# The last output tile of an attention and gMLP block in two column halves, and six earlier stores split in two

## The chip, the core and the metric

The kernel runs on one core of a Trainium2 chip. The core has five engines, each with its own queue of instructions: TensorE (PE; its weight loads are shown apart as PEld), VectorE (DVE), ScalarE (ACT), GpSimd (POOL) and SyncE (SP). Sixteen DMA engines move data between the chip's memory (HBM) and the core's (SBUF), and TensorE writes its results to a third memory, PSUM. The metric is the device time of one execution in microseconds (us), the median of several runs; less is better.

## The reference

There are two parts, one behind the other, for 4 batches of 768 positions. First attention with 8 heads of 64 columns, in which a position sees the first 4 positions and the 128 up to itself:

```python
keep = is_sink | in_window
scores = np.where(keep, scale * np.matmul(q, k.transpose(0, 1, 3, 2)), -1e9)
x = softmax(scores) @ v                        # -> [4, 768, 512]
```

Then a gated block over the attention's output `x`:

```python
h = gelu(x @ w_in)                             # [4, 768, 1024]
u, v = h[..., :512], h[..., 512:]
v_n = (v - mean(v)) / sqrt(var(v) + 1e-6) * g_ln
v_s = np.einsum('ts,bsd->btd', w_sg, v_n) + b_sg[None, :, None]
out = x + (u * v_s) @ w_out                    # float32 [4, 768, 512]
```

## The kernel before, in words

All work is written as small steps, and the string `STEPS` (lines 20 to 68) names them in the order in which they are recorded: `AV.3.1.0` is a function `AV` with the arguments 3, 1 and 0. The loop at lines 674 to 679 calls them one after the other. Nothing reorders them: each engine's queue holds its instructions in the order of the string, and the compiler's framework adds the semaphore waits that the data need. The batches overlap, so that the attention of one stands between the gated steps of the batch before it.

What the change touches is the end of a batch. A batch `b` has six output tiles `t`, of 128 positions and 512 columns each:

- `SP` (line 626, TensorE) multiplies by `w_sg`, `GT` (line 631, VectorE) scales and adds the bias, and `GM` (line 636, VectorE or GpSimd) multiplies by `u`. This gives the gated operand `wsg_gated`, one slot for three tiles.
- `OU` (line 643, TensorE) is the last product of a tile: four matmuls of 512 columns, added up in one tile `mm` of 128x512 float32 in PSUM. There are four such tiles in turn.
- `RA` (line 647, VectorE) adds `x` and writes a tile `ot` of 128x512 float32 in SBUF. There are six such tiles in turn, so an add of one batch waits until the store of the tile before in the same buffer is done.
- `ST` (line 666, SyncE) stores `ot` to the output, 256 KB in 128 rows of 2 KB.

For batch 2 the stores are recorded in the order 0, 1, 3, 2, 4, 5. For batch 3, which ends the kernel, the products are recorded in the order 3, 4, 0, 1, 2, 5, each followed by its add and its store; there is no other work left beside them.

Three functions for halves of a tile stand in the kernel already but are not called by its `STEPS`: `OH` (line 652) multiplies one half of the columns, `RH` (line 659) adds it and `SH` (line 662) stores it:

```python
    def cols(h):
        return slice(d_model // 2 * h, d_model // 2 * (h + 1))

    def OH(b, t, h):
        hf, tl = t // 3, t % 3
        ps = mm_ring["o", b, t] if h else fresh(mm_ring, ("o", b, t))
        for dc in range(KU):
            nc.tensor.matmul(ps[:, cols(h)], gated(b, hf)[:, dc, 128 * tl:128 * (tl + 1)],
                             w_out_sb[:, dc, cols(h)], start=(dc == 0), stop=(dc == KU - 1))
```

The DMAs that SyncE issues use eight completion semaphores in turn: the first DMA has number 0, the ninth has number 0 again. Each DMA instruction first waits until the DMA that had its semaphore before is done. When all steps are recorded, the framework adds closing code (shown at line 710, the launch): SyncE waits for all completion semaphores one after the other, then a barrier of all engines ends the program.

Of the kernel before, what the change touches and what calls it, by code (L numbers as in the profile page):

```python
# [58 lines left out]
MK.3.1.2.P GT.2.1.2 AV.3.1.0 NR.3.0.0 AV.3.2.0 AV.3.3.0 MK.3.0.2.P NR.3.1.0 QK.3.2.2 QK.3.3.2 EX.3.2.2 SP.2.0.2  # L59
NR.3.2.0 NR.3.3.0 EX.3.3.2 TBL.G SP.2.0.3 MK.3.2.2.P GT.2.0.2 XD.3.0 AV.3.0.1 GT.2.0.3 MK.3.3.2.P AV.3.1.1 NR.3.0.1  # L60
AV.3.2.1 GM.2.0.3.P NR.3.1.1 AV.3.3.1 SP.2.1.3 GM.2.0.2.D GM.2.1.1.P NR.3.2.1 OU.2.0 NR.3.3.1 GT.2.1.3 XD.3.1 OU.2.1
RA.2.0 GM.2.1.3.P OU.2.2 GM.2.1.2.D ST.2.0 RA.2.1 MV.3.0 RA.2.2 ST.2.1 OU.2.3 GV.3.0 OU.2.4 BN.3.0 MV.3.1 RA.2.3
RA.2.4 MV.3.2 ST.2.3 GV.3.1 ST.2.2 ST.2.4 BN.3.1 OU.2.5 GV.3.2 MU.3.2 BN.3.2 RS.3.1 MU.3.1 GU.3.2 NM.3.1 RS.3.2 NM.3.2
Z.3.0.D Z.3.1.A MU.3.0 Z.3.2.D Z.3.3.A Z.3.4.A Z.3.5.D RA.2.5 ST.2.5 SP.3.1.0 GU.3.0 SP.3.1.1 GU.3.1 GT.3.1.0 SP.3.1.2
GM.3.1.0.D GT.3.1.1 SP.3.1.3 GM.3.1.1.D GT.3.1.2 SP.3.0.0 GM.3.1.2.D SP.3.0.1 GT.3.0.0 GT.3.1.3 SP.3.0.2 GT.3.0.1
GM.3.1.3.P SP.3.0.3 GM.3.0.0.D GM.3.0.1.P GT.3.0.2 OU.3.3 GM.3.0.2.D GT.3.0.3 OU.3.4 GM.3.0.3.D RA.3.3 OU.3.0 RA.3.4
ST.3.3 OU.3.1 RA.3.0 ST.3.4 OU.3.2 ST.3.0 RA.3.1 OU.3.5 ST.3.1 RA.3.2 ST.3.2 RA.3.5 ST.3.5
"""


# [644 lines left out]
```

## Time and profile before

| what | value |
|---|---|
| three runs | 156.55, 156.59 and 156.74 us; median 156.59 |
| span of the profiled execution, first to last instruction | 154.68 us |
| SyncE's DMAs by the page: stores of the output | 24, 256 KB each, 2.3 us (median) from issue to landing |
| SyncE's DMAs: all | 49 |
| longest wait of SyncE's queue for an add (L666 for L647) | 9.8 us |
| output matmuls L643, 128x512 | 96, 379 ns recorded for one |
| adds L647, 128x512 | 24, 683 ns mean |
| granted TensorE clock, mean | 0.997 |

The profile is of one execution. Its span has its own clock, from the first instruction to the last; the runs are device times of whole executions, which is why they are longer. The three run times do not say which of them, if any, is the profiled one. A matmul's recorded time overlaps the next one's, so 379 ns is not what one costs in a row of them. "DMA to landing" is from the issue of a DMA on its queue to the last of its sixteen landings, one for each DMA engine. The view of the closing line lists event semaphores, which are waits, and drains, which wait for an engine to be empty.

### The profile page before, as it was taken

The page shows a single profiled execution, that of the slowest core. Times are in us where ns is not written, and L with a number is a line of the kernel's source. Part 1 is how long each engine was busy: PE and PEld are TensorE (multiplying, and loading weights), DVE is VectorE, ACT ScalarE, POOL GpSimd, SP SyncE. Part 2 cuts the span into 40 slices and gives each one's busy share as a digit, 9 for nine tenths or more (in the row PEclk, how much of TensorE's full clock was granted, in tenths as well). Part 3 has the DMA queues.
Part 4 walks back from the last instruction along what each step waited for, and adds up shares of the span by engine and source line. Part 5 has one row for each costly group of instructions (what it writes and reads, how often), then busy time and mean ns, then how long its engine had stood idle before and what let it go on. Part 6 is the DMA issues. An engine that isn't in the chain of part 4 may idle for free.

```text
span 154.7 us, 3863 instructions
## 1 busy us (share of the span) xinstructions
PE 147.4 (95%) x1550; PEld 94.6 (61%) x1550; DVE 123.2 (80%) x295; ACT 99.9 (65%) x117; POOL 99.3 (64%) x127
## 2 busy tenths in 40 slices
PE   6999789999999999999999999999999999999990
PEld 2455477779776776758466754585577644876530
DVE  4557789829989988897898987899799958767981
ACT  3689799699999868457987764369858022590000
POOL 4099779378999999999369769540898600400400
PEclk9999999999999999999999999999999999999998
DMA  4999999999999999999999499994610483210064
GB/s 165 295 344 157 155 195 192 169 188 190 150 144 148 186 156 173 149 154 156 157 177 252 122 277 170 192 183 58 225 72 20 86 237 112 91 72 2 0 231 177
DMA packets 86170, 24.67 MB, mean 159 GB/s; under 512 B 78660, under 2 KB 83016, under 8 KB 86152
## 3 DMA queue, kind: packets, MB, share of 16 engines
q0 software_dynamic: 64608, 11.01, 95.5%
q1 hardware_dynamic: 21544, 13.41, 32.2%
q8 instruction: 12, 0.20, 0.5%
q14 instruction: 6, 0.05, 0.1%
HBM read 24.81 MB, written 6.29 MB: 201 GB/s over the span
## 4 chain that ended last, share of the span: by engine, by line
PE 63%; POOL 18%; DMA 10%; DVE 3%; ACT 2%; issue 2%; SPq 1%; ACTq 0%
PE mm L626 17%; PE mm L643 11%; PE sc L606 10%; PE sc L565 10%; DMA v_sb<-in_v_dram 6%; POOL k L224 5%; PE sc L482 4%; DMA uT<-in_k_dram 4%; POOL q L224 4%; PE mm L523 3%; POOL wsg_gated L636 3%; PE mm L527 2%; POOL v_sb L270 2%; PE mm L381 2%; POOL P L497 2%
## 5 line engine op out<-in xcount | busy, mean ns | idle before, releaser
L487 ACT ACTIVATE P<-sc 128x1024 bf16<-128x1024 f32 (+1 forms) x48 | 43.4, 953 | 10.5 <-PE sc L482 10.4
L626 PE MATMUL mm<-wsgT,z 128*128 128x384 bf16 x192 | 34.4, 327 | 0.3 <-ACT z L596 0.3
L626 PEld LDWEIGHTS <-z 128*128 128x128 bf16 x192 | 17.6, 98 | 12.5 <-issue 0.7
L569 ACT ACTIVATE vt<-sc 128x1024 f32<-128x1024 f32 x12 | 12.3, 1026 | 18.4 <-PE sc L565 18.4
L643 PE MATMUL mm<-w_out_sb,wsg_gated 128*128 128x512 bf16 x96 | 22.7, 379 | 0.0
L631 DVE SCALAR_TENSOR_TENSOR gtmp<-mm,g_sb,b_bc 128x384 bf16<-128x384 f32 x32 | 19.0, 609 | 4.2 <-PE mm L626 4.0
L565 PE MATMUL sc<-w_in_sb,xT 128*128 128x512 bf16 x96 | 22.2, 379 | 0.0
L636 POOL TENSOR_TENSOR wsg_gated<-gtmp,uT 128x384 bf16<-128x384 bf16 x15 | 14.9, 1007 | 11.3 <-DVE gtmp L631 11.2
L606 PE MATMUL sc<-xT,w_in_sb 128*128 128x256 bf16 x192 | 22.1, 273 | 0.0
L497 POOL TENSOR_SCALAR_AFFINE_SELECT P<-P 128x512 bf16<-128x512 bf16 x21 | 13.7, 654 | 12.5 <-ACT P L487 12.5
L606 PEld LDWEIGHTS <-w_in_sb 128*128 128x128 bf16 x192 | 18.7, 98 | 3.0
L578 DVE BATCH_NORM_STATS2 st<-vt 128x6 f32<-128x512 f32 x24 | 15.4, 684 | 6.1 <-ACT vt L569 6.0
L540 DVE TENSOR_TENSOR x_sb<-mm,rcp 128x384 bf16<-128x384 f32 (+1 forms) x36 | 18.5, 513 | 1.2
L647 DVE TENSOR_TENSOR ot<-mm,x_sb 128x512 f32<-128x512 f32 x24 | 16.1, 683 | 2.0 <-PE mm L643 1.9
L587 POOL TENSOR_TENSOR rs<-rs,neg_half 128x4 f32<-128x4 f32 (+1 forms) x8 | 7.1, 883 | 15.9 <-DVE rs L582 14.5
L523 PE MATMUL mm<-v_sb,P 128*128 128x65 bf16 x192 | 15.9, 194 | 1.3 <-DMA v_sb<-in_v_dram 0.8
L224 POOL DMA_DIRECT2D k<-in_k_dram x18 | 16.4, 929 | 0.4 <-POOL wsg_gated L636 0.4
L224 POOL DMA_DIRECT2D q<-in_q_dram x18 | 16.5, 941 | 0.0
L523 PEld LDWEIGHTS <-P 128*128 128x128 bf16 x192 | 14.5, 97 | 3.2 <-issue 1.1
L611 ACT ACTIVATE uT<-sc 128x1024 bf16<-128x1024 f32 x12 | 12.2, 1022 | 5.1 <-PE sc L606 5.1
L643 PEld LDWEIGHTS <-wsg_gated 128*128 128x128 bf16 x96 | 9.2, 98 | 10.2 <-issue 0.3
L565 PEld LDWEIGHTS <-xT 128*128 128x128 bf16 x96 | 9.2, 98 | 10.1
(89 smaller groups left out, 249.4 us busy)
## 6 DMA issues: line engine op xcount, KB each, us to landing
out_dram<-ot SPq DMA_DIRECT2D x24, 256.0 KB, 2.3
v_sb<-in_v_dram POOLq DMA_DIRECT2D x8, 384.0 KB, 8.5
q<-in_q_dram POOLq DMA_DIRECT2D x18, 128.0 KB, 6.6
k<-in_k_dram POOLq DMA_DIRECT2D x18, 128.0 KB, 7.5
wsg_gated<-in_moe_w_sg_dram POOLq DMA_DIRECT2D x2, 576.0 KB, 8.4
w_in_sb<-in_moe_w_in_dram POOLq DMA_DIRECT2D x2, 512.0 KB, 10.1
uT<-in_q_dram SPq DMA_DIRECT2D x2, 384.0 KB, 3.1
uT<-in_k_dram SPq DMA_DIRECT2D x2, 384.0 KB
```

The lines of the kernel that those rows point to most:

```text
L224: return nc.gpsimd.dma_start(out=dst.rearrange("p (h d) -> p h d", h=H), in_=heads(src, b, i))
L487: nc.scalar.activation(out=P.new((b, p, g))[:, :, 0:w], in_=sc_ring[b, p, g][:, :, 0:w], func=AF.Exp, scale=scale)
L497: nc.gpsimd.affine_select(out=p4[:, :, :, 0:128], in_=p4[:, :, :, 0:128], compare_op=ALU.is_ge, fill=0.0, base=0, pattern=[[0, 2], [0, 2], ...
L523: nc.tensor.matmul(av[:, il, hl, :], pt[:, hl, c:c + 128], vb[:, h, i, :], start=first, stop=False)
L540: nc.vector.tensor_mul(x_sb.get(b)[:, i0:i0 + n, 128 * p:128 * (p + 1)].rearrange("p t (h d) -> p t h d", h=2), av[:, :, :, 0:Dh], rcp[:, ...
L565: nc.tensor.matmul(hp[:, jl, :], xT[b][:, 2 * g + jl, c, :], w_in_sb[:, c, d_half:2 * d_half], start=(c == 0), stop=(c == KD - 1))
L606: nc.tensor.matmul(hp[:, dc // 2, 256 * (dc % 2):256 * (dc % 2 + 1)], w_in_sb[:, c, 128 * dc:128 * (dc + 1)], xT[b][:, 2 * g:2 * g + 2, c, :],
L626: nc.tensor.matmul(ps[:, 0:NH], z[b][:, si, 128 * dc:128 * (dc + 1)], wsgT[:, si, NH * hf:NH * (hf + 1)], start=(si == 0), stop=(si == NT ...
L631: nc.vector.scalar_tensor_tensor(out=gtmp.new((b, hf, dc)), in0=mm_ring["g", b, hf, dc][:, 0:NH], scalar=g_sb[:, dc:dc + 1], in1=b_bc[:, N ...
L636: (nc.vector if e == "D" else nc.gpsimd).tensor_mul(gated(b, hf)[:, dc, :], gtmp[b, hf, dc], uT[b][:, dc, NH * hf:NH * (hf + 1)])
L643: nc.tensor.matmul(ps, gated(b, hf)[:, dc, 128 * tl:128 * (tl + 1)], w_out_sb[:, dc, :], start=(dc == 0), stop=(dc == KU - 1))
L647: nc.vector.tensor_add(ot.new((b, t)), mm_ring["o", b, t], x_sb[b][:, t, :])
```

## The change

Only `STEPS` changes. In batch 2 each of the six stores `ST` becomes two `SH`, one for each half of the columns, recorded one behind the other at the place of the old store. In batch 3 the last tile (tile 5) is made as two `OH`, added by two `RH` and stored by two `SH`; the two products stand one behind the other, and the first add follows the add and store of tile 2. SyncE issues 56 DMAs in place of 49. The order of all other steps stays as it is.

```diff
-RA.2.0 GM.2.1.3.P OU.2.2 GM.2.1.2.D ST.2.0 RA.2.1 MV.3.0 RA.2.2 ST.2.1 OU.2.3 GV.3.0 OU.2.4 BN.3.0 MV.3.1 RA.2.3
-RA.2.4 MV.3.2 ST.2.3 GV.3.1 ST.2.2 ST.2.4 BN.3.1 OU.2.5 GV.3.2 MU.3.2 BN.3.2 RS.3.1 MU.3.1 GU.3.2 NM.3.1 RS.3.2 NM.3.2
-Z.3.0.D Z.3.1.A MU.3.0 Z.3.2.D Z.3.3.A Z.3.4.A Z.3.5.D RA.2.5 ST.2.5 SP.3.1.0 GU.3.0 SP.3.1.1 GU.3.1 GT.3.1.0 SP.3.1.2
...
-ST.3.3 OU.3.1 RA.3.0 ST.3.4 OU.3.2 ST.3.0 RA.3.1 OU.3.5 ST.3.1 RA.3.2 ST.3.2 RA.3.5 ST.3.5
+RA.2.0 GM.2.1.3.P OU.2.2 GM.2.1.2.D SH.2.0.0 SH.2.0.1 RA.2.1 MV.3.0 RA.2.2 SH.2.1.0 SH.2.1.1 OU.2.3 GV.3.0 OU.2.4
+BN.3.0 MV.3.1 RA.2.3 RA.2.4 MV.3.2 SH.2.3.0 SH.2.3.1 GV.3.1 SH.2.2.0 SH.2.2.1 SH.2.4.0 SH.2.4.1 BN.3.1 OU.2.5 GV.3.2
+MU.3.2 BN.3.2 RS.3.1 MU.3.1 GU.3.2 NM.3.1 RS.3.2 NM.3.2 Z.3.0.D Z.3.1.A MU.3.0 Z.3.2.D Z.3.3.A Z.3.4.A Z.3.5.D RA.2.5
+SH.2.5.0 SH.2.5.1 SP.3.1.0 GU.3.0 SP.3.1.1 GU.3.1 GT.3.1.0 SP.3.1.2 GM.3.1.0.D GT.3.1.1 SP.3.1.3 GM.3.1.1.D GT.3.1.2
...
+OU.3.3 GM.3.0.2.D GT.3.0.3 OU.3.4 GM.3.0.3.D RA.3.3 OU.3.0 RA.3.4 ST.3.3 OU.3.1 RA.3.0 ST.3.4 OU.3.2 ST.3.0 RA.3.1
+OH.3.5.0 OH.3.5.1 ST.3.1 RA.3.2 ST.3.2 RH.3.5.0 SH.3.5.0 RH.3.5.1 SH.3.5.1
```

## The prediction

> **What bounds the kernel.** I read the head of the page first: which engine fills the span.
>
> ```profile
> span 154.7 us, 3863 instructions
> ...
> PE 147.4 (95%) x1550; PEld 94.6 (61%) x1550; DVE 123.2 (80%) x295; ACT 99.9 (65%) x117; POOL 99.3 (64%) x127
> ```
>
> TensorE is busy for 95% of the span, so whatever the change does beside TensorE in the middle is hidden. It must act in the tail, after the last matmul. So next I read the chain of work that ended last, for 145 to 155 us:
>
> ```profile
> 144.89 0.49 PE mm L626 x3
> 145.38 5.19 PE mm L643 x24
> 150.57 0.02 issue
> 150.59 0.69 DVE ot L647
> ```
>
> The 24 matmuls of the last six output tiles end at 150.57, and one add of 0.69 us follows. The chain stops there, at 151.28, though the span goes on to 154.68: 3.4 us come after the last computation. The view of the output tiles from 151.2 us, and the view of the closing line L710 on SyncE from 153.3 us, say what they are:
>
> ```profile
> L666 SPq DMA_DIRECT2D out_dram<-ot x1: 332/332/332, 151.3 to 151.3; - x1
> ...
> DMA to landing us min/median/max: 2.0/2.0/2.0
> ```
>
> ```profile
> L710 SPq EVENT_SEMAPHORE  x10: 17/28/28, 153.4 to 154.6; - x10
> L710 SPq DRAIN  x3: 7/7/13, 153.8 to 154.2; - x3
> ```
>
> The last store is issued at 151.313 and its sixteenth landing comes at 153.336, 2.02 us later. Then SyncE runs its closing waits: the one for the last store passes at 153.353, seven more follow 0.06 us apart, and the first drain starts at 153.847, 0.49 us after the landing was seen. From that drain to the end of the span are 0.83 us. So the tail is add 0.69, store 2.02, closing waits 0.49, final barrier 0.83.
>
> **The change part by part**, made against the span of 154.68 us. The median of the runs, 156.59 us, lies 1.91 us above it; I take this as unchanged.
>
> 1. Matmuls. Four of 512 columns become eight of 256. The new shape has a row in this trace: 48 matmuls of L606, 128x256 with a new weight load each, follow in 5.24 us, 0.109 us each. The old ones follow in 5.19 / 24 = 0.216. So 8 x 0.109 - 4 x 0.216 = +0.01 us: the last result comes at 150.60. The four extra weight loads (98 ns each on PEld) lie beside matmuls, as they do in L606; bare they would cost +0.39.
>
> 2. Adds. The order of the built program shows that the first half's add waits for TensorE and the second half's does not: TensorE counts up only once, by eight, at the eighth matmul. So the first add cannot begin while the second half is multiplied; it begins at 150.60. Its price is in the trace: L540 has 128x256 from float32 in 424 ns. So it ends at 151.02. A second add starts some 0.08 us before the first one is recorded as ended (three adds of 0.68 to 0.69 take 1.97 together), so it runs from 150.94 to 151.37, 0.09 later than the single add. On this the Trainium skill (PSUM — Partial Sum Buffer, PSUM bank collisions raise a hardware error) says to guard PSUM by bank and not by address, because TensorE writing a bank while VectorE reads it is an error. Both halves lie in one tile of 512 float32 and, by that page, in one bank; so by that rule the early start is ruled out in any build, and without it the sum would be about 0.15 us lower (third rival).
>
> 3. Issues. A store goes out 0.03 us after its add (151.28 to 151.31), so half 0 at 151.05. The next cannot follow at once: the stores at 148.29 and 148.73 stand 0.44 apart, with the second one's data ready. So half 1 goes out at 151.49, 0.18 us later than the whole tile did. No transpose stands ahead of it; the long issues of 0.83 and 0.86 us in this trace are the first stores after transposes.
>
> 4. Landing. A row becomes 1 KB in place of 2 KB. By the packet records of SyncE's queue the medians are 18 ns for 256 bytes, 27 for 512, 65 for 1536 and 85 for 2048; 1 KB is between, an estimate of 45 ns. A store is 128 rows, eight on each of 16 DMA engines, so a half saves 8 x 40 ns = 0.32 us: it lands 1.70 us after its issue, at 153.19. One DMA engine can be later: at 149.10 it takes a packet of 8192 bytes for 0.42 us (queue q14, instructions), and it ends the fifth tile's rows only at 152.35. Behind them 16 rows of 45 ns end at 153.07, and with 0.34 us from last row to landing (152.995 to 153.336 now) that is 153.41. Whether that packet comes again there is open, so I keep both ends and take the middle, 153.30: 0.04 earlier than now.
>
> 5. Closing waits. By the built program, SyncE's DMAs use eight semaphores in turn, and the closing code waits for them in the order 0 to 7. Of 49 DMAs the last is on number 0, so seven waits for long finished stores come behind it. Of 56 the last two are on 6 and 7, the last to be waited for. Behind the last landing then stands one step of 0.065 us before the drain, in place of 0.49: 0.43 us go. Nothing else is late there: VectorE's own drain ends at 151.34 and the other engines' earlier. Bounds: 0, if something unseen holds the drain, and 0.49.
>
> 6. The third batch. Six more issues of 0.39 us (the median row) and six lane waits, 2.6 us on SyncE, come between 124 and 140 us. Behind them no store is due until 147.43: SyncE's longest wait for an add is 9.8 us, and that hides them. Their data are the same bytes, while the DMA engines are at 42% (124 to 137 us) and 10% (137 to 145.2). The last batch's adds wait for these stores' buffers, which are free by about 140.1 and first wanted at 146.72. If that cover were gone it would be 0.44 us for each issue. The step is worth nothing in itself: it moves the last stores from semaphore 0 to 6 and 7.
>
> Sum: last landing 153.30, wait seen 0.02 later, one step 0.065, then 0.83: span 154.21 against 154.68, **-0.46 us, so 156.13, given as 156.1**. With the ends of step 4 it is -0.35 to -0.57, 156.0 to 156.25.
>
> **The rivals.**
>
> First, slower: an instruction block in front of the last half. The page's queue q8 carries twelve packets of 16 KB, 0.88 to 1.37 us each, on single DMA engines. The change adds 8 TensorE matmuls with 8 weight loads in place of 4 with 4, and 9 instructions on SyncE. If one more such packet falls just ahead of the last rows, the landing is that much later: 156.59 - 0.57 + 0.88 to 1.37 = 156.9 to 157.4. It decides against the change from a delay of 0.88 us on. For it: the packet at 149.10 shows that such blocks reach the tail. Against: twelve packets serve 3109 recorded TensorE instructions, the last one came at 139.07 with 2984 recorded, and the one before it at 2768; the next would be due past the 3117 of the new program. The Trainium skill (Runtime: NRT & Kernel Launch, Instruction fetch mechanics) gives blocks of 16 KiB, 256 instructions; the trace agrees (3109 / 12 = 259), which keeps this rival's chance down. Chance 0.12.
>
> Second, no difference: small rows cost what large ones do. At 85 ns a row the two halves take 1.36 us of each DMA engine. Behind the fifth tile (its rows end at 152.0 on most engines, 152.35 on the late one) the landing is 153.70 to 154.05, 0.36 to 0.71 later, against 0.43 won: 156.5 to 156.9. Against it stand the four packet sizes above; for it, that no 1 KB row is on this queue now. Chance 0.10.
>
> Third, faster still: the split works as written and half 0 is added while half 1 is multiplied. The add starts at 150.42 when the fifth tile's add ends, the stores go out at 150.89 and 151.33, half 1 lands at 153.03: 155.97. The built program's single wait speaks against it. Chance 0.04.
>
> Fourth, no difference: the closing waits are not what holds the end, and the landing alone decides: 156.59 - 0.04 = 156.55. For it: the chain view does not show these waits. Against: every step of them has its own record. Chance 0.12.
>
> **How the numbers follow.** The forecast, 156.0 to 156.25, has 0.62. This kernel's three runs lie within 0.12%, so about 0.2%, 0.31 us, can be told from no change: faster is below 156.28, slower above 156.90. Faster: 0.62 + 0.04 = 0.66. Within: 0.10 + 0.12 = 0.22. Slower: 0.12. The range takes in the forecast, the third and fourth rivals and most of the second: 155.9 to 156.75; the first stays out.
>
> **What would show it.** Step 1: last matmuls 0.109 us apart. Step 2: first 128x256 add at 150.60 and not 150.42, counted from the same start. Step 3: two issues 0.44 apart. Step 4: rows of 1 KB at 45 ns, last landing 1.7 us behind its issue. Step 5: one closing wait behind the last landing in place of eight, and a drain within 0.1 us of it. Step 6: no change on TensorE before 149.5 us. I am wrong if the last landing moves past 153.8 or the closing waits stay 0.49 us long.

## The result, and the profile after

| | before | changed |
|---|---|---|
| median of 10 runs | 156.50 us | 155.61 us |
| span of the profiled execution | 154.68 us | 154.16 us |
| fifth tile's add to the end of the span | 4.95 us | 4.48 us |

The ratio of the runs is 0.9946, with a 95% interval of 0.9925 to 0.9967: faster by 0.85 us (0.52 to 1.17). The forecast was 156.1 us, with a range from 155.9: the sign and the size of the tail came as said, the time lies below the range. One of the changed kernel's ten runs, 157.72 us at a granted clock of 0.987, is a slow one, which the median counts and the ratio does not. The profiled execution of the changed kernel took 155.89 us, so 1.73 us lie around its span.

The head of the changed kernel's page:

```profile
span 154.2 us, 3867 instructions
...
PE 145.7 (95%) x1540; PEld 94.5 (61%) x1554; DVE 122.9 (80%) x296; ACT 100.0 (65%) x117; POOL 99.7 (65%) x127
```

TensorE still fills 95%. The chain of work that ended last, 144.5 to 155 us:

```profile
145.37 4.26 PE mm L644 x19
149.63 0.89 PE mm L657 x8
150.52 0.02 issue
150.55 0.42 DVE ot L661
```

Five whole tiles (20 matmuls, of which 19 have a record) are now followed by eight matmuls of L657, and the chain goes on with the first half's add at 150.55, behind the eighth matmul. The timeline from 149 us shows the same from the other side (start, busy time, what, and what released it):

```profile
149.47 1.04 PE L657 MATMUL mm<-w_out_sb,wsg_gated 128*128 128x256 bf16 x8
...
149.67 0.69 DVE L648 TENSOR_TENSOR ot<-mm,x_sb 128x512 f32<-128x512 f32 x1 [0.17 <-PE mm L644]
150.55 0.76 DVE L661 TENSOR_TENSOR ot<-mm,x_sb 128x256 f32<-128x256 f32 x2 [0.18 <-PE mm L657]
151.00 0.84 SPq L664 DMA_DIRECT2D out_dram<-ot  x2
```

VectorE ends the fifth tile's add at 150.37 and then waits 0.18 us for TensorE. The output tiles from 150.5 us, and the closing line on SyncE from 153.2 us:

```profile
L661 DVE TENSOR_TENSOR ot<-mm,x_sb x2: 415/420/425, 150.5 to 150.9; 128x256 f32<-128x256 f32 x2
L664 SPq DMA_DIRECT2D out_dram<-ot x2: 332/376/419, 151.0 to 151.4; - x2
...
DMA to landing us min/median/max: 1.8/1.8/1.8
```

```profile
L711 SPq EVENT_SEMAPHORE  x3: 17/17/28, 153.2 to 154.1; - x3
L711 SPq DRAIN  x3: 7/7/13, 153.3 to 153.6; - x3
```

Before, ten waits stood from the last landing to the end; now there are three, one of them between the landing (153.229) and the first drain (153.313). In the tables below all times are counted from the start of the fifth tile's add (tile 2), because everything ahead of it moves as a whole from execution to execution:

| | last issue | last landing | landing to drain | end of span |
|---|---|---|---|---|
| before | 1.58 | 3.605 | 0.511 | 4.947 |
| changed | 1.75 | 3.556 | 0.084 | 4.483 |

The end comes 0.464 us earlier: 0.427 in the closing waits, 0.049 in the landing, and -0.012 in what follows the drain.

### The profile page after: what moved, and what is told of

Its sections match the earlier page's. It is cut to its first block, busy times and chain, and to the rows that moved or that the text cites. A ratio compares the mean times of both kernels' runs of the same rounds, so it can differ in the third digit from the quotient of the medians.

```text
span 154.2 us, 3867 instructions
## 1 busy us (share of the span) xinstructions
PE 145.7 (95%) x1540; PEld 94.5 (61%) x1554; DVE 122.9 (80%) x296; ACT 100.0 (65%) x117; POOL 99.7 (65%) x127
## 4 chain that ended last, share of the span: by engine, by line
PE 54%; POOL 18%; DMA 15%; ACT 4%; DVE 4%; issue 2%; SPq 1%; DVEq 0%; ACTq 0%; POOLq 0%
PE mm L627 15%; DMA v_sb<-in_v_dram 11%; PE mm L644 10%; PE sc L566 9%; PE sc L607 8%; POOL q L225 5%; POOL k L225 4%; DMA uT<-in_k_dram 4%; PE sc L483 4%; PE mm L524 3%; POOL v_sb L271 3%; PE mm L528 2%; POOL wsg_gated L637 2%; POOL P L498 2%; POOL P L501 2%
## 5 line engine op out<-in xcount | busy, mean ns | idle before, releaser
L644 PE MATMUL mm<-w_out_sb,wsg_gated 128*128 128x512 bf16 x85 | 21.2, 379 | 0.5
L648 DVE TENSOR_TENSOR ot<-mm,x_sb 128x512 f32<-128x512 f32 x23 | 15.4, 683 | 2.2 <-PE mm L644 2.2
L524 PE MATMUL mm<-v_sb,P 128*128 128x65 bf16 x192 | 16.1, 194 | 0.6 <-DVE x_sb L541 0.4
L528 PE MATMUL mm<-v_sb,P 128*128 128x65 bf16 x160 | 15.4, 193 | 0.4 <-POOL P L501 0.4
```

Source lines behind the costliest of these rows:

```text
L524: nc.tensor.matmul(av[:, il, hl, :], pt[:, hl, c:c + 128], vb[:, h, i, :], start=first, stop=False)
L528: nc.tensor.matmul(av[:, il, hl, :], pt[:, hl, c:c + 128], vb[:, h, i - 1, :], start=False, stop=(i < 2 and il == n - 1 and hl == 1))
L644: nc.tensor.matmul(ps, gated(b, hf)[:, dc, 128 * tl:128 * (tl + 1)], w_out_sb[:, dc, :], start=(dc == 0), stop=(dc == KU - 1))
```

## The experiments

The theory: the time goes in the tail, and there because the last store's semaphore stands last in the closing order. The first rival: the halves do it (smaller rows, an earlier first store). The second: the six splits in batch 2 do something earlier in the program. The third: the tail gives 0.47 us, and what the runs show beyond it is their own scatter.

### One more DMA: the halves stay, the closing order goes back

```diff
-... RA.3.4 ST.3.3 OU.3.1 ...
+... RA.3.4 SH.3.3.0 SH.3.3.1 OU.3.1 ...
```

> The changed kernel with one more store split (tile 3 of batch 3), so SyncE issues 57 DMAs and the last half store is on semaphore 0 again; halves as in the changed kernel. Theory A (the place of the last store among the closing waits decides): seven closing waits stand behind the last landing again, drain 0.49 us after it, time within 0.1 us of the kernel before, 0.4 us above the changed kernel. Theory B (the smaller, halved last tile decides): as fast as the changed kernel, 0.5 us or more below the kernel before. Theory C (part of the gain of the medians, some 0.4 us, arises before the last batch's tail): 0.4 us below the kernel before although the closing waits are back.

SyncE issues 57 DMAs, the last on semaphore 0. The closing line on SyncE, from 153.7 us:

```profile
L711 SPq EVENT_SEMAPHORE  x10: 17/28/28, 153.8 to 155.0; - x10
L711 SPq DRAIN  x3: 7/7/13, 154.3 to 154.6; - x3
```

The ten waits are back, landing to drain is 0.511 us again, and the end stands at 4.877, 0.07 before the kernel before. Runs: 156.24 us, ratio 0.9988 (0.9963 to 1.0013). With the old closing order nearly nothing is left of the gain, though halves and splits are all there.

### The same number of DMAs, the last tile whole

```diff
-OH.3.5.0 OH.3.5.1 ST.3.1 RA.3.2 ST.3.2 RH.3.5.0 SH.3.5.0 RH.3.5.1 SH.3.5.1
+OU.3.5 ST.3.1 RA.3.2 ST.3.2 RA.3.5 ST.3.5
```

with `ST.3.3` as two halves, as above.

> 56 DMAs with the last tile whole: six stores of batch 2 and one early store of batch 3 split, last store of 256 KB on semaphore 7. Theory A: one closing wait behind the last landing, drain 0.07 us after it, 0.40 to 0.45 us below the kernel before. Theory B: no gain, within 0.1 us of the kernel before. Theory C: 0.8 us below the kernel before, with only 0.4 of it in the tail of the trace.

The closing line from 154.25 us:

```profile
L711 SPq EVENT_SEMAPHORE  x3: 17/17/28, 154.3 to 155.2; - x3
L711 SPq DRAIN  x3: 7/7/13, 154.4 to 154.7; - x3
```

Three waits with a whole last tile: landing to drain 0.081, end at 4.532, 0.415 earlier than before. Runs: 155.90 us, 0.9974 (0.9944 to 1.0004), an interval that takes in no change; it is the tail that tells here. By it the closing order alone carries nine tenths of the gain.

### The halves alone: batch 2 stored whole

```diff
-SH.2.0.0 SH.2.0.1 ... SH.2.5.0 SH.2.5.1
+ST.2.0 ... ST.2.5
```

> The last tile in halves alone, batch 2 stored whole: 50 DMAs, last half on semaphore 1. Theory A: six closing waits behind the last landing, drain 0.43 us after it, 0.1 us below the kernel before at most. Theory B: 0.5 us or more below the kernel before. Theory C: 0.4 to 0.5 us below with nothing in the tail.

Fifty DMAs, the last on semaphore 1. The closing line from 153.5 us, and what the DMA queues carried from 149 to 149.6 us (queue, kind: packets, MB, share of 16 engines):

```profile
L711 SPq EVENT_SEMAPHORE  x9: 17/28/28, 153.6 to 154.8; - x9
```

```profile
q1 hardware_dynamic: 90, 0.15, 71.7%
q14 instruction: 1, 0.01, 4.5%
```

Nine waits, 0.446 us from landing to drain, 0.065 less than with one more behind. The halves land at 3.668, later than the whole tile of before: the packet of 8192 bytes on queue q14 (0.43 us on one DMA engine) that the prediction found at 149.10 stands here at 149.27, ahead of the last rows. Of the sixteen landings of the last half, one for each DMA engine, fifteen come by 3.54 and one 0.12 later. End at 4.944, 0.003 from before; runs 156.49 us, 1.002 (0.999 to 1.005). The same window of the changed kernel has no such packet; it is found at 133 to 134 us:

```profile
q1 hardware_dynamic: 120, 0.23, 102.4%
```

```profile
q14 instruction: 1, 0.01, 3.1%
```

So the splits in batch 2 do two things: they turn the closing order, and they bring this packet out of the tail. In all four profiles with 49 or 50 DMAs the last two such packets stand at 140.6 to 141.8 us and at 149.1 to 150.0; in the fourteen others, in which SyncE issues 54 to 57, they stand at 132.0 to 134.9 and at 139.9 to 142.2, and none comes later. That they fetch SyncE's own instructions is inferred from this, not shown.

### The changed kernel and the kernel before, again

Four more times the changed kernel as it is, and twice the kernel before against itself, to see what the comparison gives where nothing is changed.

> The changed kernel once more, beside the three others on one chip. Theories A and B: 0.46 to 0.52 us below the kernel before, as the two profiled executions (154.68 and 154.16 us of span) have it. Theory C: 0.8 to 0.9 us below, as the medians of ten runs had it (156.50 and 155.61).

> The changed kernel a third time. Theory A (the whole effect is the tail, 0.46 to 0.48 us by the profiled executions, and the 0.85 of the first series came from the scatter of the first 60 us): 0.3 to 0.6 us below the kernel before, ratio near 0.997, interval over that. Theory C (a real further gain ahead of the tail): 0.8 us or more, ratio at 0.995 or below.

> The kernel before, unchanged, as a control. Theory A (the series differ by the scatter of the first 60 us alone): within 0.3 us of the other runs of the same kernel, the interval over 1. If kernels measured in this place come out faster whatever they are, it is 0.2 us or more below its own other runs.

> The changed kernel beside two controls on one chip. Theory A: 0.3 to 0.6 us below the controls and below the kernel before. Theory C (a gain ahead of the tail): 0.7 to 0.9 us below both.

> The control again, the kernel before unchanged: by theory A within 0.3 us of the other runs of the same kernel, the interval over 1.

> The changed kernel again, beside the controls: theory A 0.3 to 0.6 us below them, theory C 0.7 to 0.9.

| kernel | median, us | ratio and interval | last landing | landing to drain | end |
|---|---|---|---|---|---|
| changed, first | 155.61 | 0.9946 (0.9925 to 0.9967) | 3.556 | 0.084 | 4.483 |
| changed, second | 155.94 | 0.9972 (0.9950 to 0.9994) | 3.546 | 0.084 | 4.474 |
| changed, third | 156.14 | 0.9940 (0.9907 to 0.9974) | 3.546 | 0.084 | 4.474 |
| changed, fourth | 155.88 | 0.9962 (0.9927 to 0.9997) | 3.544 | 0.083 | 4.466 |
| changed, fifth | 155.74 | 0.9965 (0.9937 to 0.9992) | 3.551 | 0.084 | 4.463 |
| before, again | 156.07 | 1.0004 (0.9969 to 1.0039) | 3.621 | 0.510 | 4.963 |
| before, again | 156.00 | 0.9996 (0.9962 to 1.0030) | 3.740 | 0.510 | 5.098 |

The ratios show no bias of the comparison (1.0004 and 0.9996), as far as intervals of 0.35% on either side can tell. Not all came as expected. By their medians the two controls lie 0.31 and 0.38 us below the 35 runs of the same kernel beside them, where at most 0.3 was expected, and the changed kernel's fourth and fifth series lie 0.12 to 0.33 below the controls, where 0.3 to 0.6 was. The third series by itself met the mark set for a further gain ahead of the tail (0.995 or below). Medians of twelve runs scatter that much: by the means, the 24 runs of the changed kernel's last two series lie 0.48 us (0.18 to 0.78) below the 24 of the controls.

The tail of the changed kernel is the same within 0.02 us in five profiles. That of before is not: in the last row the store lands 2.16 us after its issue in place of 2.02. The q14 packet of that execution, in the window from 149 to 150.5 us:

```profile
q1 hardware_dynamic: 269, 0.49, 89.9%
q14 instruction: 1, 0.01, 1.3%
```

It comes 0.2 us later than in the other two profiles of before. There, too, one of the fifth tile's sixteen landings is 0.2 late, but that DMA engine catches up before the last tile's rows begin; here it doesn't, and fifteen landings of the last store come by 3.61, the sixteenth at 3.74.

Over the profiles the tail is 5.003 us (mean of three) before and 4.472 (mean of five) after: -0.53, 0.9966 of 156.4 us. The five ratios, weighted by their intervals, give 0.9958, within some 0.0012: -0.66 us, -0.47 to -0.84. The two agree, the tail at the near end of that interval. The runs alone would leave room for a remainder of up to 0.3 us ahead of the tail. The tail starts at 150.20 us before (mean of 149.73, 150.57, 150.31) and at 150.02 after (149.48 to 150.76), a difference far below what single executions spread over. But the profiles show where that spread lies. From VectorE's 141st instruction (at 67.6 to 70.0 us) to the start of the tail, 81.28 to 81.29 us pass in the three profiles of before and 81.28 to 81.33 in the five of the changed kernel. So the changed kernel gains nothing there, and ahead of 124 us the two programs have the same steps. The second rival, a gain earlier in the program, falls with this; what the single series show beyond the tail is scatter.

### Two PSUM tiles, and a half on ScalarE's queue

The first add waits for all eight matmuls because both halves lie in one tile. Give each half its own (`RH` then reads the half's tile):

```diff
-ps = mm_ring["o", b, t] if h else fresh(mm_ring, ("o", b, t))
+ps = fresh(mm_ring, ("o", b, t, h))
```

> The changed kernel with each half of the last tile in a PSUM tile of its own, so that the first half's add waits for four matmuls and not for eight. Theory D (TensorE's release of the one tile held the first add): the first add begins when the fifth tile's add ends, 0.15 to 0.18 us earlier against the matmuls; SyncE then issues the halves 0.44 us apart behind the fifth store, so the last landing and the time come 0.10 us earlier than in the changed kernel. Rival S (SyncE's issues alone set the end): the adds come earlier and the stores do not, no gain beyond 0.03 us.

The second half's store waits for the first one's issue. Give it to another queue:

```diff
-nc.sync.dma_start(out=..., in_=...)
+(nc.scalar if h and b == 3 else nc.sync).dma_start(out=..., in_=...)
```

> The changed kernel with the last half store issued by ScalarE, which is idle there. Theory S (SyncE's 0.44 us from issue to issue holds back the second half): its issue comes 0.03 us behind its add, 0.10 us earlier than in the changed kernel, and so does the end. Rival (the issue is not what it waits for, or ScalarE's issues take longer to land): no gain or a loss of up to 0.3 us.

And both:

> Both edits: own PSUM tiles and the last half issued by ScalarE. That store then has completion semaphore 6, with number 7 waited for behind it. Theories D and S together: last issue 0.20 us earlier than in the changed kernel, one closing step of 0.06 us given back, 0.14 us below the changed kernel and 0.6 us below the kernel before.

| | first half's add | last issue | last landing | issue to landing | end |
|---|---|---|---|---|---|
| changed | 0.873 | 1.751 | 3.556 | 1.805 | 4.483 |
| two PSUM tiles | 0.608 | 1.641 | 3.514 | 1.873 | 4.427 |
| half on ScalarE's queue | 0.873 | 1.659 | 3.516 | 1.857 | 4.444 |
| both | 0.608 | 1.384 | 3.512 | 2.128 | 4.486 |

The output tiles of the kernel with both, from 150.9 us:

```profile
L664 SPq DMA_DIRECT2D out_dram<-ot x1: 407/407/407, 151.3 to 151.3; - x1
L664 ACTq DMA_DIRECT2D out_dram<-ot x1: 372/372/372, 151.5 to 151.5; - x1
...
DMA to landing us min/median/max: 2.0/2.1/2.1
```

The last issue moves by 0.37 us, the last landing by 0.04: the issue is not what holds it. Runs: 155.90 us, 0.9945 (0.9913 to 0.9977); 155.94 us, 0.9966 (0.9944 to 0.9988); 156.08 us, 0.9966 (0.9944 to 0.9989). None differs from the changed kernel by what can be told. All three were expected 0.10 to 0.14 us earlier than it, and missed that: the ends come 0.056 and 0.039 earlier and 0.003 later. With both, the half on ScalarE's queue has semaphore 6, so one closing step stands behind it again.

### The closing order once more, with the halves on semaphores 0 and 7

`ST.1.2` as two halves, on top of the kernel with both: ScalarE's half comes on semaphore 7, SyncE's half 0 on semaphore 0.

```diff
-... SP.2.0.1 ST.1.2 MK.3.3.1.P ...
+... SP.2.0.1 SH.1.2.0 SH.1.2.1 MK.3.3.1.P ...
```

> As the run before with one store of batch 1 split too, so that ScalarE's last half has semaphore 7, the last waited for. By theory A it is 0.06 us below the run before, 0.20 us below the changed kernel and 0.65 us below the kernel before; by the rival (the place among the closing waits does not matter) the same as the run before.

The closing line from 152.1 us:

```profile
L711 SPq EVENT_SEMAPHORE  x10: 17/28/28, 152.1 to 153.4; - x10
L711 SPq DRAIN  x3: 7/7/13, 152.6 to 152.9; - x3
```

A miss: the end was expected earlier and came at 4.534, 0.05 later than with both. Half 0 lands only at 3.18; SyncE waits for semaphore 0 first, so the seven steps behind it begin there and end at 3.63, past the last landing (3.504). It isn't the last landing alone that counts, but for each store its landing plus 0.061 us for every semaphore behind it. The runs, 155.40 us, 0.9926 (0.9899 to 0.9953), are the best ratio of all kernels, while the end is the latest of the four variants of the tail (4.427, 4.444, 4.486, 4.534): a series of six runs can be off by more than these differ.

### What holds the last landing

If the sixteen DMA engines' rows hold it, it must come earlier when tile 2's store is left out, and only where the issue is early.

> The run with own PSUM tiles and the last half by ScalarE, with tile 2 of batch 3 not stored at all (its part of the output is left out). Theory R: with those rows gone the last half lands 1.8 us after its issue and not 2.13, that is 3.2 us behind the start of tile 2's add in place of 3.51. Rival I: 2.1 us after its issue as before, 3.5.

> The changed kernel with tile 2 of batch 3 not stored (its part of the output is left out). Theory R: little changes, since the last half is issued late there and landed after 1.80 us already: 3.50 to 3.55 us behind the start of tile 2's add. If those rows do hold it up, it lands after 1.70 us as the prediction had it, at 3.45.

Both leave out `ST.3.2`. With both variants the last landing comes at 3.150 (with the store 3.512), 1.764 us after its issue; in the changed kernel at 3.507 (with it 3.556), 1.756 after. The first one's output tiles from 149.4 us:

```profile
L664 SPq DMA_DIRECT2D out_dram<-ot x1: 333/333/333, 150.0 to 150.0; - x1
L664 ACTq DMA_DIRECT2D out_dram<-ot x1: 369/369/369, 150.3 to 150.3; - x1
...
DMA to landing us min/median/max: 1.8/1.8/1.8
```

Without tile 2's rows the last half lands 1.76 us after its issue from either queue. So in the kernel with both, tile 2's store costs it 0.36 us; in the changed kernel only 0.05. Of these 0.049 us, 0.036 lie in the issue itself: its record is 419 ns long with tile 2's store and 383 without, and from its end to the landing are 1.386 and 1.373 us. What makes the second issue longer than the 332 ns of the others is not known. Would it help to bring the rows in sooner? The last two tiles in halves, on SyncE's and ScalarE's queues in turn (`RW` adds a half of a whole product, `SH.2.0` is whole again, so that the last SyncE store has the last semaphore):

```diff
-RA.3.2 ST.3.2 RH.3.5.0 SH.3.5.0 RH.3.5.1 SH.3.5.1
+RW.3.2.0 SH.3.2.0 RW.3.2.1 SH.3.2.1 RH.3.5.0 SH.3.5.0 RH.3.5.1 SH.3.5.1
```

> The last two tiles halved: tile 2 is added and stored in halves too, tile 5 has its own PSUM tile for each half, the halves are issued in turn by SyncE and ScalarE, and batch 2 has five split stores, so there are 56 DMAs and the last half has semaphore 7. Theory R (in the tail the 16 DMA engines take the rows of the last stores back to back, so that an early issue of the last half alone is worth nothing, and the rows must start earlier): tile 2's first half is issued 0.27 us earlier than its whole store was, the last landing comes 0.3 to 0.4 us earlier than in the changed kernel (3.55 us behind the start of tile 2's add there), the time is 0.3 to 0.4 below the changed kernel, 0.75 to 0.85 below the kernel before. Rival I (ScalarE's issues take longer to land): the last landing stays at 3.5 us, no gain against the changed kernel.

Landings of the four halves: 2.302, 2.670, 3.041, 3.417, 0.37 us apart, which is eight rows of 46 ns on each DMA engine. The end is at 4.345, 0.14 before the changed kernel's and less than was expected, since the rows now queue behind tile 1's store (landed at 1.90). Runs: 155.81 us, 0.9968 (0.9935 to 1.0001): the 0.14 us can't be told by runs.

## Why the prediction missed the time, point by point

1. **Matmuls**: right. They follow 0.109 us apart, and the add behind them starts 0.01 later than the whole tile's did.
2. **Adds**: right. The first half's add stood at 0.873, behind the eighth matmul, and not at 0.69, where the fifth tile's add ended. The second started 0.34 after it, as said. The working given for it, three adds in 1.97 us, has two overlaps and so 0.04 for each, not the 0.08 used; but the first two of those adds do overlap by 0.08, and so do the halves (0.084). With two PSUM tiles the first half's add started at 0.608 while TensorE still multiplied, so the single tile is what holds it. On this the Trainium skill (PSUM — Partial Sum Buffer, PSUM bank collisions raise a hardware error) says that engines on different banks run clean beside each other; the 0.608 agrees with that. Whether a read beside a write in one bank fails, as it also says, no run here shows. The 0.15 us of the third rival did not come with it either: 0.27 us at the add were 0.04 at the landing.
3. **Issues**: right, 0.425 us apart against 0.44; the last issue 0.17 later against 0.18.
4. **Landing**: the sum came out (0.05 earlier against 0.04), but by luck: it was the middle between a landing with the packet on q14 and one without. Rows of 1 KB take 46 ns (estimate 45). The packet was not there, and still the landing took 1.805 us, not 1.70. The saving by smaller rows was right: from the end of the issue's record to the landing it is 1.386 us, where the whole tile took 1.691, 0.305 less against the 0.32 summed. What the prediction lacked is the issue's record, 419 ns for the second half against 332 for the whole tile.
5. **Closing waits**: right, 0.427 against 0.43. One step is 0.061 to 0.065 us by 0.511 with seven behind, 0.446 with six, and 0.08 with none.
6. **The third batch**: hidden, as said; nothing moved on TensorE. "Worth nothing in itself" was not quite so: without these splits the q14 packet stands in the tail, and costs 0.12 us there in the kernel with halves alone and 0.13 in one of three profiles of before.

**The sum** of the tail, -0.46, was measured as -0.464 in the two profiles, and as -0.53 over all of them.

**The step that failed** is the base and its scatter: "The median of the runs, 156.59 us, lies 1.91 us above it; I take this as unchanged", and with it "three runs lie within 0.12%", which left the scatter of a series out of the range. The mechanism and the tail's sum were right. In the later profiles 1.70 to 1.74 us lie around a span, so the execution of 154.68 us took some 156.4 and not 156.59: from there the same sum gives 155.9. And the runs spread far more than three showed: single runs of before from 155.1 to 157.8 us, medians of its series from 156.00 to 156.83.

The miss of 0.52 us, from 156.13 to 155.61, has three parts. The base was 0.18 too high: 119 runs of before, in the four series with the changed kernel and their two controls, have a mean of 156.41 us. The tail gives 0.53 us over all profiles where 0.46 was summed, 0.07 more. From there the expected time is 155.88, and the remaining 0.27 is the scatter of the first series, whose interval for the gain (0.52 to 1.17) takes in 0.53. The range should have been wider by such an interval, some 0.3 us on either side.

Where that scatter arises can be read: the programs are the same up to 124 us, yet VectorE's 141st instruction starts at 68.45 us before, at 68.37 in the changed kernel, and from 67.6 to 69.96 in the other profiles. From there to the tail all eighteen profiles take 81.28 to 81.44 us. The chain of work from 0 to 62 us, in the kernel before and in the changed one:

```profile
8.79 8.73 DMA v_sb<-in_v_dram
```

```profile
8.48 8.04 DMA v_sb<-in_v_dram
...
42.11 9.21 DMA v_sb<-in_v_dram
```

The start waits for loads of `v`, which took 8.0 and 8.7 us here, and at 42 us such a load stands in the chain of one of the two only. That the loads make the scatter is inferred from these two chains, not shown.

The rivals: the packet of 16 KB ahead of the last rows did not come (twelve such packets as before), nor did rows of 1 KB cost like 2 KB ones. That the closing waits do not count was refuted by the whole last tile with 56 DMAs, -0.415 us.

## What to carry to other kernels

Read what follows the last landing as closely as what precedes it: with completion semaphores waited for one after the other, a store should end on a later one the later it lands, and the number of earlier DMAs decides that. Before moving an issue forward, look whether the rows ahead of it on the DMA engines let it land earlier. And take the spread of a time from several series: three runs that lie close together give neither its base nor its scatter.

## What the runs showed of the hardware

- A closing wait whose store is long done costs 0.061 to 0.065 us on SyncE, so the number of a semaphore was worth up to 0.43 us.
- A packet of instructions (8192 bytes, 0.43 us on one DMA engine) in the tail held one of sixteen landings, and so the last store, back by 0.12 us with the halves alone, where rows follow rows, and by 0.13 in one of three profiles of before; in the other two the gap ahead of the last store took it up. The Trainium skill (Runtime: NRT & Kernel Launch, Instruction fetch mechanics) gives refills of 16 KiB and calls the cost of crossing a block mostly hidden; queue q8's twelve packets agree in size, q14's do not, and this one's cost was not hidden in all executions.
- Without another tile's rows ahead, the last half of 128 KB landed 1.76 us after its issue by SyncE and by ScalarE alike. Four halves issued 0.33 us apart landed 0.37 us apart, eight rows of 46 ns for each DMA engine.
- Eighteen executions spread over 2.35 us in their first 68 us, and agree within 0.16 us over the 81 us behind that.
